# A small last block of an expert's tokens: high and low halves side by side in one stationary operand

## The chip, the core and the metric

The kernel runs on one core of one Trainium2 chip. The metric is the device time of one execution in microseconds (us). TensorE (PE) multiplies, VectorE (DVE) and ScalarE (ACT) compute element by element, GpSimd (POOL) here mostly issues indirect DMAs, and SyncE (SP) issues the other DMAs. Each engine works through its own instruction stream in order and waits on semaphores for the others.

## The reference

Three stages, fp32 throughout: sliding-window attention with sink tokens over 1,536 tokens, a mixture of 8 experts (one expert per token, at most 384 tokens each), and a feed-forward layer with squared ReLU. The change is in the second stage:

```python
expert_idx = np.argmax(x @ w_gate, axis=1)
for i in range(N):                       # capacity = N // E * 2 = 384
    e = expert_idx[i]
    if counts[e] < capacity:
        disp[e, counts[e]] = x[i]; pos[i] = counts[e]; counts[e] += 1; keep[i] = True
h = np.maximum(np.einsum('ecd,edf->ecf', disp, w1), 0.0)   # 512 -> 1024
y = np.einsum('ecf,efd->ecd', h, w2)                       # 1024 -> 512
out[i] = gate_w[i] * y[expert_idx[i], pos[i]]              # for the kept tokens
```

With the reference's inputs the experts 0 to 7 get 290, 123, 98, 163, 117, 165, 92 and 488 tokens; the last is cut to 384.

## The kernel before

**Precision.** A matmul in fp32 is made of passes on rounded operands. Every operand is split into a high part (its value rounded to the matmul format, a copy on ACT) and a low part (the rest, a subtraction on DVE). A product is three passes: high by high, high by low, low by high.

**Blocks.** An expert's tokens are taken in blocks of 128. `body(e, b, ...)` computes block `b` of expert `e`: `g1` makes the hidden layer in two halves of 512 columns (L859; the 128 tokens are the stationary operand, the weights stream past, 512 columns to a matmul), `relu` brings each half to SBUF (L862, ACT), `tr` transposes it by four matmuls (L870) and splits the result (L873 ACT, L874 DVE), and `g2` multiplies by the second weight (L885). A full block is 24 matmuls of `g1` and 24 of `g2`, 512 columns each, with eight transposes between. At the end DVE scales `y` by the gate (L916) and POOL scatters it to `yd` in DRAM (L917).

**Order.** The order of every engine's instructions is written out by hand in `body`. Expert `e`'s first block carries the splitting of expert `e+1`'s weights: sixteen pairs of a copy (L145, ACT) and a subtraction (L146, DVE), spread by the plan `HEAVY`; the eight last stand at the end, behind the preparation `pre` of the next blocks' tokens (L831 PE, L834 ACT, L835 DVE). A raw weight's buffer is free, and SP fetches the next (L139), when its two subtractions are done.

**Later blocks.** `more(e, b)` computes block `b` of 1 and 2 only if the expert has more than `128 b` tokens, which each engine decides by a branch of its own (L927). It splits no weights and prepares the tokens of block `b+1` (if `b+1` is under 3) whether that block is needed or not. Banks of PSUM: three for `h` (`s`), one for the transposes (`pt`), one for `y` (`ot`).

**After the experts.** The feed-forward layer runs in chunks of 512 tokens (L1050, L1106); the last chunk's length is chosen by branches too (L1147).

Of the kernel before, what the change touches and what calls it, by code (L numbers as in the profile page):

```python
# [8 lines left out]
F32 = mybir.dt.float32  # L9
F32R = mybir.dt.float32r  # L10
BF16 = mybir.dt.bfloat16
I32 = mybir.dt.int32
AF = mybir.ActivationFunctionType
ALU = mybir.AluOpType
AX = mybir.AxisListType

P = 128
# [5 lines left out]
LIGHT = (1, 1, 1, 1, 1, 1)  # L23
# [10 lines left out]
def kernel(  # L34
# [15 lines left out]
    nc = tc.nc  # L50
    B, H, S, D = q.shape
    NTOK, DM = out.shape
    E = w_gate.shape[1]
    F = w1.shape[2]
    FF = w_in.shape[1]
    HP = H // 2
    KD = DM // P
    NF = F // P
# [28 lines left out]
    def ps(tag, name):  # L87
        banks[tag].append(banks[tag].pop(0))
        return psum.tile([P, 512], F32, tag=f"b{banks[tag][-1]}", name=name)
# [123 lines left out]
    yd = dram.tile([NTOK, DM + 1], F32, name="yd")  # L213


    W = {0: Weights(0, wx, "x"), 1: Weights(1, None, "y")}
# [60 lines left out]
    ident = const.tile([P, P], F32, name="ident")  # L277
# [43 lines left out]
    if fast:  # L321
# [22 lines left out]
        for g in range(3 if stack else 1):  # L344
            x = own[g * HS : (g + 1) * HS]
            nc.gpsimd.affine_select(x, x, pattern=[[-NS, H], [0, D]], compare_op=ALU.is_ge, fill=0.0, base=0, channel_multiplier=1)
            nc.gpsimd.affine_select(x, x, pattern=[[NS, H], [0, D]], compare_op=ALU.is_ge, fill=0.0, base=NS - 1, channel_multiplier=-1)
    else:
        for j in range(NJ):
            m = ap_.tile([P, S], F32, name=f"m{j}")  # L350
# [268 lines left out]
    def route(n):  # L619
        need(n, "oh")  # L620
        if nblk == 0:
            return
        d = blk[n]
        p_ = ps("lg" if n < NQB - 2 else "s", "pos")
        nc.tensor.matmul(p_[:, :E], tri, d["oh"], start=True, stop=False)
        nc.tensor.matmul(p_[:, :E], ones, runoh, start=False, stop=True)
        nc.gpsimd.tensor_add(runoh, runoh, d["oh"])
        pj = small("pj", E)
        pos = small("pos", 1)
        at = ap_.tile([P, capp], BF16, tag="at", name="at", bufs=2)  # L630

        def places():
            nc.vector.tensor_scalar(at, place, pos, None, op0=ALU.is_equal)
            d["at"] = at

        def take():
            nc.vector.tensor_tensor_reduce(
                out=pj, in0=p_[:, :E], in1=d["oh"], scale=1.0, scalar=0.0, op0=ALU.mult, op1=ALU.add, accum_out=pos
            )
            short.insert(0, places)  # L640

        late.append(take)

    def invert(n):
        if nblk == 0:
            return
        need(n, "at")
        at, wh = blk[n]["at"], blk[n]["wh"]
        p_ = ps("lg" if n < NQB - 2 else "s", "inv")
        for b in range(nblk):  # L650
            for t in range(2):
                nc.tensor.matmul(p_[:, b * E : (b + 1) * E], at[:, b * P : (b + 1) * P], wh[:, t, :], start=t == 0, stop=t == 1)
        late.append(lambda: nc.vector.tensor_add(inv, inv, p_[:, : nblk * E]))
        blk.pop(n)


    XB = 3
    xring = {}
    for b in range(XB):
        for i in range(2):  # L660
            t_ = xring[b, i] = xrp.tile([P, DM + 1], F32, name=f"xb{b}{i}")
# [30 lines left out]
    for n in range(NQB):  # L692
# [5 lines left out]
        fs = (lambda n=n: row(n, 0), lambda n=n: row(n, 1), lambda n=n: route(n), lambda n=n: invert(n))  # L698
# [18 lines left out]
    for u in range(len(units) + PL + 1):  # L717
# [4 lines left out]
        if u < len(units):  # L722
            n, c = units[u]
            b, j = divmod(n, NJ)
# [16 lines left out]
        m, c = divmod(u, HP)  # L741
# [30 lines left out]
    if nblk:  # L772
        src = xrp.tile([P, nblk, E], I32, name="src")
# [5 lines left out]
        p_ = ps("lg", "cnt")  # L779
# [12 lines left out]
        dst = const.tile([P, nblk, E], I32, name="dst")  # L792
# [9 lines left out]
    mp = moe.__enter__()  # L802
# [5 lines left out]
    xT = {}  # L808
# [3 lines left out]
    def x_at(e, b):  # L812
        return xring[min(b, XB - 1), e % 2]

    def gate_at(e, b):
        return gate[2 + b % 2 if b else e % 2]

    def load_x(e, b):
        if e >= E or b >= nblk:
            return  # L820
        nc.gpsimd.indirect_dma_start(
            out=x_at(e, b), out_offset=None, in_=xd[:, :], in_offset=bass.IndirectOffsetOnAxis(ap=src[:, b, e : e + 1], axis=0),
            bounds_check=NTOK - 1, oob_is_err=False,
        )

    def pre(e, b):
        if e >= E or b >= nblk:
            return
        p_ = ps("bg", "xT")
        for c in range(KD):  # L830
            nc.tensor.transpose(p_[:, c * P : (c + 1) * P], x_at(e, b)[:, c * P : (c + 1) * P], ident)  # L831
        xT[e, b] = xTs[min(b, 1)]
        h_, l_ = (x.rearrange("p c n -> p (c n)") for x in xT[e, b])
        nc.scalar.copy(h_, p_)  # L834
        nc.vector.tensor_sub(l_, p_, h_.bitcast(F32))  # L835
        g_ = gate_at(e, b)
        nc.vector.tensor_scalar(g_, x_at(e, b)[:, DM:], 1e-9, None, op0=ALU.add)
        nc.vector.reciprocal(g_, g_)

    def body(e, b, splits, plan, also):  # L840
        xh, xl = xT[e, b]
        wts = W[e]
        splits = list(splits)

        def sp(n):
            for _ in range(n):
                if splits:
                    splits.pop(0)()

        hs = mp.tile([P, F], F32, tag="hs", name="hs", bufs=1)  # L850
        hp = [None, None]

        def g1(half, ks):
            if ks[0] == 0:
                hp[half] = ps("s" if half or b else "iv", "h")
            for kk in ks:
                r = slice(half * 512, half * 512 + 512)
                for m, (a, bb) in enumerate(((xh, wts.h), (xh, wts.l), (xl, wts.h))):
                    nc.tensor.matmul(hp[half], a[:, kk, :], bb[kk][:, r], start=(kk == 0 and m == 0), stop=(kk == KD - 1 and m == 2))  # L859

        def relu(half):
            nc.scalar.activation(hs[:, half * 512 : half * 512 + 512], hp[half], AF.Relu)  # L862

        hT = [None, None]

        def tr(half):
            p_ = ps("pt", "hT")
            for c in range(4):
                o0 = half * 512 + c * P
                nc.tensor.transpose(p_[:, c * P : (c + 1) * P], hs[:, o0 : o0 + P], ident)  # L870
            h_ = mp.tile([P, 512], F32R, tag="hTh", name="hTh", bufs=2)
            l_ = mp.tile([P, 512], F32R, tag="hTl", name="hTl", bufs=2)
            nc.scalar.copy(h_, p_)  # L873
            nc.vector.tensor_sub(l_, p_, h_.bitcast(F32))  # L874
            hT[half] = (h_, l_)

        y = ps("ot", "y")

        def g2(fs):
            for f in fs:  # L880
                h_, l_ = (x[:, (f % 4) * P : (f % 4 + 1) * P] for x in hT[f // 4])
                wh, wl = wts.h[KD + f // 2], wts.l[KD + f // 2]
                r = slice((f % 2) * 512, (f % 2) * 512 + 512)
                for m, (a, bb) in enumerate(((h_, wh), (h_, wl), (l_, wh))):
                    nc.tensor.matmul(y, a, bb[:, r], start=(f == 0 and m == 0), stop=(f == NF - 1 and m == 2))  # L885

        def point(i):
            for f in also.get(i, ()):
                f()

        plan = iter(plan)
        g1(0, [0, 1, 2, 3])
        sp(next(plan))
        relu(0)
        g1(1, [0, 1])
        sp(next(plan))
        tr(0)
        g1(1, [2, 3])
        sp(next(plan))
        relu(1)  # L900
        point(0)
        g2([0, 1])
        sp(next(plan))
        tr(1)
        point(1)
        g2([2, 3])
        point(2)
        sp(next(plan))
        g2([4, 5])
        point(3)  # L910
        g2([6, 7])
        point(4)
        sp(next(plan))
        y_ = mp.tile([P, DM + 1], F32, tag="ys", name="ys", bufs=2)
        nc.gpsimd.tensor_copy(y_.bitcast(I32)[:, DM:], src[:, b, e : e + 1])
        nc.vector.tensor_scalar(y_[:, :DM], y, gate_at(e, b), None, op0=ALU.mult)  # L916
        nc.gpsimd.indirect_dma_start(  # L917
            out=yd[:, :], out_offset=bass.IndirectOffsetOnAxis(ap=dst[:, b, e : e + 1], axis=0), in_=y_, in_offset=None,
            bounds_check=NTOK - 1, oob_is_err=False,
        )  # L920
        sp(len(splits))

    def more(e, b):

        if b >= nblk:
            return
        with tc.If(vals[e] > b * P):  # L927
            if b + 1 >= XB:
                load_x(e, b + 1)
            body(e, b, [], LIGHT, {3: [lambda: pre(e, b + 1)]})  # L930
            more(e, b + 1)

    NPRE = 2
    order = [("i", f) for f in range(NPRE)]
# [53 lines left out]
    vals = []  # L988
    if nblk > 1:
        vals = [nc.values_load(cnt[0:1, e : e + 1], min_val=0, max_val=cap) for e in range(E)]  # L990
# [205 lines left out]
```

## Time and profile before

| | |
|---|---|
| three runs | median 614.15 us (613.76 to 614.29) |
| the profiled execution, its own time | 615.59 us |
| its span, first to last instruction | 613.9 us |
| busy share of the span: PE, DVE, ACT, POOL | 94%, 58%, 48%, 22% |
| mean granted TensorE clock | 0.983 |
| blocks of tokens computed | 14: eight first ones, six later ones |

The profiled execution took 615.59 us, of which 613.9 are its span; 1.7 us lie around it. Matmuls overlap in the array: a row's busy time of a matmul (0.4 us) is longer than the distance from its start to the next one's start, and it is the starts that count time. In a row of the timeline the first two numbers are start and duration, and a bracket at the end tells how long the engine had idled before and what released it.

### The profile page before, as it was taken

The page shows a single profiled execution, that of the slowest core. Times are in us where ns is not written, and L with a number is a line of the kernel's source. Part 1 is how long each engine was busy: PE and PEld are TensorE (multiplying, and loading weights), DVE is VectorE, ACT ScalarE, POOL GpSimd, SP SyncE. Part 2 cuts the span into 40 slices and gives each one's busy share as a digit, 9 for nine tenths or more (in the row PEclk, how much of TensorE's full clock was granted, in tenths as well). Part 3 has the DMA queues.
Part 4 walks back from the last instruction along what each step waited for, and adds up shares of the span by engine and source line. Part 5 has one row for each costly group of instructions (what it writes and reads, how often), then busy time and mean ns, then how long its engine had stood idle before and what let it go on. Part 6 is the DMA issues. An engine that isn't in the chain of part 4 may idle for free. (4 is left out here: it accounts for less than half of the span.)

```text
span 613.9 us, 9330 instructions
## 1 busy us (share of the span) xinstructions
PE 577.7 (94%) x3231; PEld 457.4 (75%) x3231; DVE 353.2 (58%) x833; ACT 296.2 (48%) x649; POOL 135.8 (22%) x235
## 2 busy tenths in 40 slices
PE   8999999969999999999699899999999999999992
PEld 4778778737887787777577677788888888888881
DVE  3788888736439966957652799994223223322221
ACT  4888878616348756747341556563212222222220
POOL 8444554232223422422111100000200000200002
PEclk9999999988999999999899899999999999999997
DMA  9698995445428995857763646621100000100001
GB/s 191 156 219 161 215 198 141 139 138 171 154 60 248 325 309 160 263 208 222 221 218 114 207 146 197 208 84 51 69 0 18 0 1 0 73 0 2 1 0 59
DMA packets 74624, 82.07 MB, mean 134 GB/s; under 512 B 42200, under 2 KB 53464, under 8 KB 74560
## 3 DMA queue, kind: packets, MB, share of 16 engines
q1 hardware_dynamic: 70608, 72.45, 41.6%
q0 software_dynamic: 3952, 8.82, 4.2%
q8 instruction: 34, 0.56, 0.4%
q14 instruction: 30, 0.25, 0.1%
HBM read 69.29 MB, written 16.08 MB: 139 GB/s over the span
## 5 line engine op out<-in xcount | busy, mean ns | idle before, releaser
L1052 ACT ACTIVATE xb<-a 128x512 f32<-128x512 f32 (+1 forms) x48 | 27.5, 573 | 151.7 <-PE a L1050 151.7
L1053 DVE TENSOR_TENSOR xb<-xb 128x512 f32<-128x512 f32 (+1 forms) x48 | 31.7, 661 | 115.6 <-ACT xb L1052 115.5
L1106 PE MATMUL out<-yh,gh 128*128 128x512 f32 (+1 forms) x192 | 77.1, 401 | 0.6 <-ACT gh L1067 0.5
L1106 PE MATMUL out<-yl,gh 128*128 128x512 f32 (+1 forms) x192 | 76.6, 399 | 0.0
L1106 PE MATMUL out<-yh,gl 128*128 128x512 f32 x176 | 70.4, 400 | 2.4 <-DVE gl L1069 2.1
L451 ACT ACTIVATE p<-p,nm 128x260 f32<-128x260 f32 (+2 forms) x96 | 46.8, 489 | 17.3 <-DVE nm L439 16.2
L917 POOL DMA_INDIRECT yd<-ys,dst x14 | 25.5, 1821 | 119.2 <-POOLq L927 51.1
L1075 POOL DMA_INDIRECT out_dram<-raw,tok x12 | 11.7, 976 | 176.0 <-DVE raw L1116 115.3
L1050 PE MATMUL a<-x2Ah,xh 128*128 128x512 f32 (+1 forms) x128 | 48.1, 376 | 0.3 <-PEq L1020 0.3
L1050 PE MATMUL a<-x2Al,xh 128*128 128x512 f32 (+1 forms) x128 | 47.9, 374 | 0.2 <-DVEq L1020 0.2
L1050 PE MATMUL a<-x2Ah,xl 128*128 128x512 f32 (+1 forms) x128 | 47.8, 374 | 0.0
L146 DVE TENSOR_TENSOR yl<-raw,yh 128x512 fp32r<-128x512 f32 x64 | 40.4, 687 | 7.8 <-ACT yh L145 7.8
L1069 DVE TENSOR_TENSOR gl<-xb,gh 128x512 fp32r<-128x512 f32 (+1 forms) x48 | 31.1, 649 | 22.1 <-ACT gh L1067 20.8
L1106 PEld LDWEIGHTS out<-yh,gl 128*128 128x128 f32 x176 | 33.4, 190 | 12.6 <-DVE gl L1069 4.2
L1106 PEld LDWEIGHTS out<-yh,gh 128*128 128x128 f32 (+1 forms) x192 | 35.6, 185 | 9.6 <-ACT gh L1067 0.9
L1106 PEld LDWEIGHTS out<-yl,gh 128*128 128x128 f32 (+1 forms) x192 | 35.5, 185 | 8.4
L1067 ACT CAST gh<-xb 128x512 fp32r<-128x512 f32 (+1 forms) x48 | 28.6, 596 | 24.3 <-DVE xb L1053 24.3
L145 ACT CAST yh<-raw 128x512 fp32r<-128x512 f32 x64 | 35.4, 625 | 2.6 <-PEq L927 1.7
L145 ACT CAST xh<-raw 128x512 fp32r<-128x512 f32 x64 | 36.2, 619 | 0.5 <-DMA raw<-in_moe_w_dram 0.2
L874 DVE TENSOR_TENSOR hTl<-hT,hTh 128x512 fp32r<-128x512 f32 x28 | 19.3, 690 | 28.1 <-ACT hTh L873 25.5
L146 DVE TENSOR_TENSOR xl<-raw,xh 128x512 fp32r<-128x512 f32 x48 | 30.1, 687 | 1.9 <-ACT xh L145 1.8
L526 PE MATMUL ot<-pts,v 128*64 128x128 f32 x352 | 30.1, 286 | 0.5 <-ACT pts L493 0.5
(204 smaller groups left out, 1399.1 us busy)
## 6 DMA issues: line engine op xcount, KB each, us to landing
raw<-in_moe_w_dram SPq DMA_DIRECT2D x64, 512.0 KB, 5.2
raw<-in_moe_w_in_dram SPq DMA_DIRECT2D x16, 512.0 KB, 5.4
raw<-in_moe_w_out_dram SPq DMA_DIRECT2D x8, 1024.0 KB
yd<-zero SPq DMA_DIRECT2D x12, 256.5 KB, 6.3
xd<-x SPq DMA_DIRECT2D x12, 256.5 KB, 5.8
xb<-yd SPq DMA_DIRECT2D x12, 256.5 KB, 3.3
kr<-in_k_dram SPq DMA_DIRECT2D x12, 256.0 KB, 4.7
qr<-in_q_dram SPq DMA_DIRECT2D x12, 256.0 KB, 7.1
```

Of the source, the lines that this page charges most:

```text
L145: (hi or nc.scalar.copy)(self.h[i][:, sl], t[:, sl])
L146: (eng or nc.vector).tensor_sub(self.l[i][:, sl], t[:, sl], self.h[i].bitcast(F32)[:, sl])
L451: nc.scalar.activation(d["p"][:, h, :width], d["p"][:, h, :width], AF.Exp, bias=d["nm"][:, h : h + 1], scale=-1.0, accum_out=d["sm"][:, h ...
L526: nc.tensor.matmul(d["o"][i * D : (i + 1) * D, c * P : (c + 1) * P], vt[b, kb][:, h, :], t_, start=i not in d["started"], stop=False, skip ...
L874: nc.vector.tensor_sub(l_, p_, h_.bitcast(F32))
L917: nc.gpsimd.indirect_dma_start(out=yd[:, :], out_offset=bass.IndirectOffsetOnAxis(ap=dst[:, b, e : e + 1], axis=0), in_=y_, in_offset=None ...
L1050: nc.tensor.matmul(a_[:, :w], a, bb[:, kk, :w], start=(kk == 0 and m == 0), stop=(kk == KD - 1 and m == 2))
L1052: nc.scalar.activation(r_, a_[:, :w], AF.Relu)
L1053: nc.vector.tensor_mul(r_, r_, r_)
L1067: nc.scalar.copy(gh[:, :w], r_)
L1069: nc.vector.tensor_sub(gl[:, : w - k_], r_[:, : w - k_], gh.bitcast(F32)[:, : w - k_])
L1106: nc.tensor.matmul(o, a, bb[:, r], start=(f == 0 and m == 0), stop=(f == NFF - 1 and m == len(prods) - 1))
```

## The change

`more` now asks a second question. A later block that holds more than 64 tokens goes through `body` as before. One with at most 64 goes through the new `packed_body`. It uses that only 64 of the 128 columns of the stationary operand hold tokens: ACT copies the low parts of the 64 tokens into the other 64 columns, beside the high parts, and each weight pass (high, then low) multiplies both at once. The result has the products of the high parts in the upper 64 rows and those of the low parts in the lower 64 rows. Between the two layers the halves are transposed and added by DVE (`tensor_reduce`, L952), put through ReLU into the high part by ACT (L953), and the rest becomes the low part on DVE (L954); at the end ACT copies the lower half of `y`, and DVE adds the upper (L979, L980) and scales (L981). The preparation of a block `b+1` is left out.

```diff
+    def packed_body(e, b):
+        (x, xl), wts = xT[e, b], W[e]
+        nc.scalar.copy(x[:, :, P // 2 :], xl.bitcast(F32)[:, :, : P // 2])
...
+            for kk in ks:
+                for m, bb in enumerate((wts.h, wts.l)):
+                    nc.tensor.matmul(
+                        hp[half], x[:, kk, :], bb[kk][:, r], start=(kk == 0 and m == 0), stop=(kk == KD - 1 and m == 1)
+                    )
...
+        def tr(half):
+            p_ = ps("pt", "hT")
+            for c in range(4):
+                o0 = half * 512 + c * P
+                nc.tensor.transpose(p_[:, c * P : (c + 1) * P], hs[:, o0 : o0 + P], ident)
+            pv = p_.rearrange("p (c t n) -> p c n t", c=4, t=2)
...
+            nc.vector.tensor_reduce(sm, pv, axis=AX.X, op=ALU.add)
+            nc.scalar.activation(t_[:, :, 0, :], sm, AF.Relu)
+            nc.vector.scalar_tensor_tensor(
+                t_[:, :, 1, :], in0=sm, scalar=0.0, in1=t_.bitcast(F32)[:, :, 0, :], op0=ALU.max, op1=ALU.subtract
+            )
...
+        g1(0, [0, 1, 2, 3])
+        keep(0)
+        g1(1, [0, 1, 2])
+        tr(0)
+        g1(1, [3])
+        keep(1)
+        g2([0, 1, 2])
+        tr(1)
+        g2([3, 4, 5, 6, 7])
...
+        nc.scalar.copy(y_[:n, :DM], y[n:, :])
+        nc.vector.tensor_add(y_[:n, :DM], y_[:n, :DM], y[:n, :])
+        nc.vector.tensor_scalar(y_[:n, :DM], y_[:n, :DM], gate_at(e, b)[:n], None, op0=ALU.mult)
...
     def more(e, b):
         if b >= nblk:
             return
         with tc.If(vals[e] > b * P):
-            if b + 1 >= XB:
-                load_x(e, b + 1)
-            body(e, b, [], LIGHT, {3: [lambda: pre(e, b + 1)]})
-            more(e, b + 1)
+            with tc.If(vals[e] > b * P + P // 2) as cmp:
+                if b + 1 >= XB:
+                    load_x(e, b + 1)
+                body(e, b, [], LIGHT, {3: [lambda: pre(e, b + 1)]})
+                more(e, b + 1)
+            with cmp.Else():
+                packed_body(e, b)
```

The first place is ACT's order where expert 3's first block ends and its second begins (`xh` are expert 4's weights being split, `hs` and `hTh` the hidden layer, `xT1h` and `xT1l` the block's tokens). Before:

```order
L145 CAST xh_3642<-raw_75 128x512
L927 COMPARE_AND_BRANCH
L862 ACTIVATE hs<-h 128x512 [waits PE_49,Activation_49]
L873 CAST hTh<-hT 128x512 [waits DVE_49,PE_49]
L862 ACTIVATE hs<-h 128x512 [waits PE_49]
L873 CAST hTh<-hT 128x512 [waits DVE_49,PE_49,Activation_49]
L834 CAST xT1h<-xT 128x512 [waits DVE_49,PE_49,Activation_49]
```

And now the same place; of the packed way's rows, which stand further on in the program:

```order
L927 CAST xT1h<-xT1l 128x4x64 [waits DVE_49,Activation_49]
L942 COPY hs<-h 128x512 [waits PE_49]
L953 ACTIVATE hTh<-hsum 128x4x64 [waits DVE_49]
L942 COPY hs<-h 128x512 [waits PE_49]
L953 ACTIVATE hTh<-hsum 128x4x64 [waits DVE_49]
L979 COPY ys<-y 64x512 [waits DMASW5_49,DMASW3_49,DMASW6_49,DMASW1_49,DMASW7_49,PE_49,Pool_49]
L992 UNCONDITIONAL_BRANCH
```

Before, ACT's first work for the block was `relu`, behind the first half of `g1`; now it is the copy of the low parts, ahead of `g1`. The copy stands behind the eight L145 of the first block. The second place is PE's order between the halves of the same block, from the first transposes to the first matmuls of `g2` (`yh`, `yl` are expert 3's weights). Before:

```order
L870 MATMUL hT<-ident,hs 128x128 [waits Activation_49]
L870 MATMUL hT<-ident,hs 128x128 x3
L859 MATMUL h<-yh_3304,xT1h 128x512
L859 MATMUL h<-yl_3305,xT1h 128x512
L859 MATMUL h<-yh_3304,xT1l 128x512
L859 MATMUL h<-yh_3306,xT1h 128x512
L859 MATMUL h<-yl_3307,xT1h 128x512
L859 MATMUL h<-yh_3306,xT1l 128x512
L885 MATMUL y<-yh_3308,hTh 128x512 [waits DVE_49,Activation_49]
L885 MATMUL y<-yl_3309,hTh 128x512
L885 MATMUL y<-yh_3308,hTl 128x512 [waits DVE_49]
```

And now:

```order
L948 MATMUL hT<-ident,hs 128x128 [waits Activation_49]
L948 MATMUL hT<-ident,hs 128x128 x3
L937 MATMUL h<-yh_3578,xT1h 128x512
L937 MATMUL h<-yl_3579,xT1h 128x512
L965 MATMUL y<-yh_3580,hTh 128x512 [waits DVE_49]
L965 MATMUL y<-yl_3581,hTh 128x512
```

Between the transposes and the first matmul that needs what DVE made of them stood eight matmuls, six of them of `g1` (the first two of `g2` needed only ACT's part); now two stand there. The second half is alike: two matmuls of `g2` between its transposes and the wait.

## Rows read from the trace of the kernel before

**Rows 1.** The profile's chain of waits that ended last, shares by engine and line.
```profile
PE out L1106 20%; PE a L1050 19%; DVE raw L184 1%; PE x2T L969 1%; DMA out_dram<-raw,tok 1%; DVE gl L1069 0%; DVE raw L182 0%; ACT xb L1052 0%; POOLq L1190 0%; POOL out_dram L1075 0%; DVE raw L1112 0%; ACT raw L1111 0%; DVE yl L189 0%; DVE raw L185 0%; DVE xb L1053 0%
```
**Rows 2.** Line L917, one scatter a block: count, duration, first and last start.
```profile
L917 POOL DMA_INDIRECT yd<-ys,dst x14: 983/1904/2652, 156.5 to 336.5; - x14
```
**Rows 3.** Windows of three later blocks: length, then PE, PEld, DVE, ACT, POOL busy, PEclk, DMA.
```profile
165.77:177.84 12.07, 12.07 (x58) 9.80 (x57) 2.41 (x6) 3.93 (x7) 1.19 (x2) 1.00 0.06 23
220.33:233.43 13.10, 12.66 (x62) 10.00 (x60) 7.34 (x14) 5.45 (x11) 2.73 (x2) 1.00 0.67 213
261.25:274.35 13.10, 12.66 (x62) 10.01 (x60) 7.35 (x14) 5.45 (x11) 2.73 (x2) 1.00 0.67 233
```
**Rows 4.** PE's timeline, expert 3's second block: start, duration, engine, line, operation.
```profile
220.33 0.39 PE L859 MATMUL h<-yh,xT1h 128*128 128x512 f32 x1
...
222.90 0.39 PE L859 MATMUL h<-yh,xT1l 128*128 128x512 f32 x1
...
224.53 0.60 PE L870 MATMUL hT<-ident,hs 128*128 128x128 f32 x4
224.88 0.48 PE L859 MATMUL h<-yh,xT1h 128*128 128x512 f32 x1
...
225.20 0.39 PE L859 MATMUL h<-yl,xT1h 128*128 128x512 f32 x1
...
232.59 0.40 PE L885 MATMUL y<-yh,hTl 128*128 128x512 f32 x1
...
233.43 0.50 PE L859 MATMUL h<-xh,xT0h 128*128 128x512 f32 x1 [0.44 <-PEq L927]
```
**Rows 5.** ACT's and DVE's timeline beside it.
```profile
218.24 4.27 ACT L145 CAST xh<-raw 128x512 fp32r<-128x512 f32 x8
223.39 0.60 ACT L862 ACTIVATE hs<-h 128x512 f32<-128x512 f32 x1 [0.87 <-PE h L859]
225.16 0.58 ACT L873 CAST hTh<-hT 128x512 fp32r<-128x512 f32 x1 [1.18 <-PE hT L870]
225.78 0.69 DVE L874 TENSOR_TENSOR hTl<-hT,hTh 128x512 fp32r<-128x512 f32 x1 [0.60 <-ACT hTh L873]
```
**Rows 6.** ACT's timeline at expert 5's second block.
```profile
259.17 4.27 ACT L145 CAST xh<-raw 128x512 fp32r<-128x512 f32 x8
```
**Rows 7.** DVE ahead of expert 0's third block, PE behind it.
```profile
165.23 0.69 DVE L835 TENSOR_TENSOR xT1l<-xT,xT1h 128x512 fp32r<-128x512 f32 x1 [2.56 <-ACT xT1h L834]
177.84 0.39 PE L859 MATMUL h<-yh,xT0h 128*128 128x512 f32 x1
```
**Rows 8.** Groups by line and form: count, busy us, mean ns, idle before.
```profile
L585 ACT COPY x<-xr 128x256 f32<-128x256 f32 x24 | 8.8, 368 | 4.7 <-DVE lt L580 4.6
L495 DVE COPY pts<-pt 128x512 f32<-128x512 f32 x19 | 13.0, 685 | 0.2 <-PE pt L489 0.2
L495 DVE COPY pts<-pt 128x256 f32<-128x256 f32 x4 | 1.7, 419 | 0.3 <-PE pt L489 0.3
L611 DVE TENSOR_REDUCE lg<-lt 128x8 f32<-128x64 f32 x12 | 3.2, 263 | 0.0
L185 DVE SCALAR_TENSOR_TENSOR raw<-raw 128x1024 int32<-128x1024 int32 x16 | 19.6, 1226 | 0.5
```
**Rows 9.** PE's timeline behind its three longest waits from 140 us on.
```profile
296.76 0.50 PE L885 MATMUL y<-yh,hTl 128*128 128x512 f32 x1 [1.83 <-DVE hTl L874]
303.00 0.72 PE L969 MATMUL x2T<-ident,xb 128*128 128x128 f32 x4 [2.77 <-DMA xb<-yd]
...
344.87 0.79 PE L1106 MATMUL out<-yh,gl 128*128 128x512 f32 x1 [2.13 <-DVE gl L1069]
```
**Rows 10.** Windows of the low clock behind the second of them, columns as in Rows 3.
```profile
303.40:306.80 3.40, 3.40 (x13) 2.71 (x12) 0.69 (x1) 0.58 (x1) 0.37 (x2) 0.51 1.01 315
```
**Rows 11.** PE's timeline across the branches at L1147.
```profile
526.50 0.39 PE L1106 MATMUL out<-yh,gl 128*128 128x512 f32 x1
526.72 0.35 PE L1050 MATMUL a<-x2Ah,xh 128*128 128x416 f32 x1
```

More of the change, by code (lines that the diff above doesn't have):

```diff
@@ L921, in body, with g1, keep, g2 @@
         sp(len(splits))
+    def packed_body(e, b):
+        (x, xl), wts = xT[e, b], W[e]
+        nc.scalar.copy(x[:, :, P // 2 :], xl.bitcast(F32)[:, :, : P // 2])
+        hs = mp.tile([P, F], F32, tag="hs", name="hs", bufs=1)
+        hp, hT = [None, None], [None, None]
+        def g1(half, ks):
+            if ks[0] == 0:
+                hp[half] = ps("s", "h")
+            r = slice(half * 512, half * 512 + 512)
+            for kk in ks:
[3 more added lines that the diff above has]
+                    )
+        def keep(half):
+            nc.scalar.copy(hs[:, half * 512 : half * 512 + 512], hp[half])
+        def tr(half):
[4 more added lines that the diff above has]
+            pv = p_.rearrange("p (c t n) -> p c n t", c=4, t=2)
+            sm = mp.tile([P, 4, P // 2], F32, tag="hTl", name="hsum", bufs=2)
+            t_ = mp.tile([P, 4, 2, P // 2], F32R, tag="hTh", name="hTh", bufs=2)
+            nc.vector.tensor_reduce(sm, pv, axis=AX.X, op=ALU.add)
[3 more added lines that the diff above has]
+            )
+            hT[half] = t_.rearrange("p c t n -> p c (t n)")
+        y = ps("ot", "y")
+        def g2(fs):
+            for f in fs:
+                r = slice((f % 2) * 512, (f % 2) * 512 + 512)
+                for m, bb in enumerate((wts.h[KD + f // 2], wts.l[KD + f // 2])):
+                    nc.tensor.matmul(y, hT[f // 4][:, f % 4, :], bb[:, r], start=(f == 0 and m == 0), stop=(f == NF - 1 and m == 1))
+        g1(0, [0, 1, 2, 3])
[7 more added lines that the diff above has]
+        g2([3, 4, 5, 6, 7])
+        n = P // 2
+        y_ = mp.tile([P, DM + 1], F32, tag="ys", name="ys", bufs=2)
+        nc.gpsimd.tensor_copy(y_.bitcast(I32)[:n, DM:], src[:n, b, e : e + 1])
+        nc.scalar.copy(y_[:n, :DM], y[n:, :])
+        nc.vector.tensor_add(y_[:n, :DM], y_[:n, :DM], y[:n, :])
+        nc.vector.tensor_scalar(y_[:n, :DM], y_[:n, :DM], gate_at(e, b)[:n], None, op0=ALU.mult)
+        nc.gpsimd.indirect_dma_start(
+            out=yd[:, :], out_offset=bass.IndirectOffsetOnAxis(ap=dst[:n, b, e : e + 1], axis=0), in_=y_[:n, :], in_offset=None,
+            bounds_check=NTOK - 1, oob_is_err=False,
+        )
```

## The prediction

> **What bounds the kernel now.** I read the chain of waits first, then line L917 and windows over three blocks, then the timelines of PE, ACT and DVE inside one block, and the groups by form for the new operations. The chain that ended last is PE at the feed-forward layer's two matmul lines, with little else [rows 1]: what PE loses or wins among the experts moves the end by as much, as long as PE is the bound there too. It is. Fourteen scatters mean fourteen blocks, so six later ones [rows 2]; the counts that the reference's router gives (290, 163 and 165 tokens at experts 0, 3 and 5; 384 at the last) put at most 64 tokens into exactly three of them: expert 0's third (34), expert 3's second (35) and expert 5's second (37). In their windows PE is busy 12.07 us of 12.07, and 12.66 of 13.10, at full clock [rows 3]. The reader is to see that PE waits for nothing inside these blocks, and that DVE and ACT have time to spare there.
>
> **What is removed.** From 220.33 to 222.90 eleven matmuls start, one every 0.234 us [rows 4]; the 0.39 us of a row overlap and count nothing. A full block has 48 of 512 columns, a packed one 32: 16 x 0.234 = 3.74 us less. Experts 3 and 5 also lose the needless preparation of a third block, four transposes: 0.35 us to the next start, and 0.09 since the first matmul behind transposes takes 0.32 to the next for 0.23 [rows 4], 0.44 together. Their not-taken branch behind the block goes too: 232.59 to 233.43 is 0.84, 0.61 over the pitch [rows 4]. A packed block ends in an unconditional branch, as expert 0's third did, and behind that one PE ran on without a wait [rows 7].
>
> **What is added at the entry.** PE's first matmul now waits for ACT's copy of the low parts. At expert 3 PE could start at 220.33 [rows 4], but ACT is still splitting expert 4's weights: eight copies from 218.24 for 4.27 us, to 222.51 [rows 5]. Before this hid, since ACT's first work for the block, `relu`, came at 223.39, 0.49 after PE's last matmul of the half, with 0.87 us of idle ahead of it. The copy is 256 elements a row: 0.37 us by the ACT copy of 128x256 [rows 8]. With 0.04 for a handover (225.16 + 0.58 to 225.78 [rows 5]) PE starts at 222.92: 2.59 us late. What queues behind the copy on ACT is `keep`, for the transposes, which are later by as much. Expert 5 is the same picture, ACT busy from 259.17 for 4.27 [rows 6] against a block start at 261.25 [rows 3]: 2.60. At expert 0 ACT splits nothing; the low part it copies is ready at 165.92 [rows 7], so PE starts at 165.92 + 0.04 + 0.37 + 0.04 = 166.37 for 165.77 [rows 3]: 0.60. Each restart costs 0.09 more.
>
> **What is added between the layers.** Before, the chain from transposes to the low part ran beside eight matmuls. Now two stand there, twice in a block. The chain: 0.63 from the first transpose to the next engine's start (224.53 to 225.16 [rows 4, 5]); DVE's reduce of 512 elements from PSUM; ACT's ReLU of 256; DVE's rest of 256; three handovers of 0.04. No row shows such a reduce. From below it is 0.26 (a reduce of 64 elements), from above 1.23 (1024 elements); I take 0.69, the DVE copy of 128x512 out of PSUM, which reads as much [rows 8]. The Trainium skill ("VectorE: DVE Perf Modes", "The perf-mode tier table" and "Rules for kernel authors") gives the reduce only the slowest rate of one element a cycle and calls it the slowest operation to have on a hot path; the row of 64 elements is too small to tell rates, and by the rule the sum stays at 0.69 and its lower end is out of reach. ReLU: 0.37, rest: 0.42, as the copies of 256 elements [rows 8]. Sum 0.63 + 0.69 + 0.37 + 0.42 + 0.12 = 2.23. Beside it run the transposes and two matmuls, 0.35 + 0.32 + 0.23 = 0.90 [rows 4]. So PE waits 1.33 us and restarts for 0.09, 1.42 a time, 2.84 a block. From below (both of DVE's at 0.26) the wait is 0.59 shorter, 0.74; from above (reduce at 1.23) 1.87.
>
> **What lies beside.** The end of a packed block is longer by an ACT copy (0.6) and a DVE pass (0.7), both after PE's last matmul. Behind them stand the first three splits of the next expert's weights; PE first needs those engines when twelve matmuls and six more are through, 4.2 us later, and three splits on DVE take 2.1. Hidden; if not, 0.7 us a block. SP's fetches start later by as much, from buffers filled long before. The second question is one more branch an engine; a branch cost PE nothing where it ran on [rows 7].
>
> **The sum.** Expert 3: -3.74 - 0.44 - 0.61 + 2.59 + 0.09 + 2.84 = +0.73. Expert 5: +0.74. Expert 0: -3.74 + 0.60 + 0.09 + 2.84 = -0.21. Together +1.3 us: 13.3 removed, 14.6 given back in waits.
>
> **The clock.** PE's new idle of 2.6 us at two places is among those behind which the granted clock fell: it fell to half behind waits of 2.77 and 2.13 us, and stayed full behind one of 1.83 [rows 9]; behind the first of these it read 0.51 for 3.4 us [rows 10]. Half of 3.4 us is lost at most, 1.7; I take 1.6, as PE has matmuls for most of it. I give each of the two places 4 in 10, so the likeliest case is none or one fall, and I carry half a fall, 0.8.
>
> **The forecast.** The profiled execution took 615.59 us, 613.9 of span and 1.7 around it; 615.59 + 1.3 + 0.8 = 617.7. The median of the runs shown is 1.44 under that execution: 616.2 us, slower by 0.3%. Its own range, none or one fall and 0.15 a wait either way, is 614.5 to 617.9.
>
> **Rivals.**
> - *Two falls of the clock.* 614.15 + 1.3 + 3.2 = 618.7. For it: the two entries look alike in the trace. Against: 1.83 kept the clock, and 2.6 is not far over.
> - *Branches cost.* The program grows, and the packed way lies behind the block it replaces, so each of three jumps to it and four skips of a whole expert (1, 2, 4, 6) goes further. If a far target held PE for another 0.44 us, the largest wait for its own sequencer [rows 4], seven would add 3.1: 618.5 with half a fall left out. Against it: behind the branches at L1147, which pass over two whole variants of the last chunk, PE kept its pitch, 526.50 to 526.72 [rows 11]. The Trainium skill ("Runtime: NRT & Kernel Launch", "Instruction fetch mechanics") says that a taken branch beyond the loaded pages stalls on a fetch of instructions; at L1147 the trace does not agree, so the rival keeps a small chance.
> - *The halves are cheap: faster.* Its place is the wait between the layers, six times. With no fall of the clock and a chain shorter by 0.22 us a time, the change is worth nothing; from 0.42 on it is faster by over 0.2%. At the lower bound (0.59 a time) it is 1.3 - 3.5 = -2.2: 612.0. For it: small operations in the rows are cheap. Against: the reduce must read 512 elements.
> - *The new way is not taken* (the tokens of a block not counted as I do): two questions for one, 614.2.
>
> **How the numbers follow.** Two places at 4 in 10 give none, one or two falls 36, 48 and 16 in 100. The three share 0.71: the forecast has 0.60 (none 0.26, one 0.34), two falls 0.11. Branches have 0.08, cheap halves 0.14, not taken 0.07. 0.2% is 1.23 us, about what a measurement here can tell from no change: slower means over 615.38. Without a fall 615.4 lies on that line, so half of the 0.26 counts as slower, and nearly all of the 0.34: 0.47, with the two slow rivals 0.66. Faster is under 612.92: 0.09 of the cheap halves. The rest, 0.25, is no change. The range for 8 in 10 leaves out the ends: 613.0 to 619.0.
>
> **What would show it.** Right: in the changed profile the first L937 of experts 3 and 5 idles 2.4 to 2.7 us, released by ACT's copy L927; L965 idles about 1.3 us twice in each of three blocks, released by DVE L954; L952 takes about 0.7; the windows of the three blocks are 13.8, 13.8 and 11.9 us from end to start of the neighbours' matmuls. A granted clock of 0.5 behind an entry would show a fall. Wrong: L965 idle under 1.0 (cheap halves), idle put down to PE's own sequencer at L991 or L992 (branches), no L937 at all, or a longer expert 1, 4 or 6, which would mean that the block's longer end is not hidden.

## The result: slower by 1.5%, and the profile after

| | before | after |
|---|---|---|
| median of the timed runs | 613.95 us | 622.2 us (621.4 to 625.7) |
| ratio, 95% interval | 1 | 1.0147, 1.0107 to 1.0187 |
| the profiled execution, its span | 615.59, 613.9 us | 621.4, 619.6 us |

One run of the kernel after, disturbed by a low clock throughout (657.3 us), is left out. The change costs about 9 us; 2.1 were forecast, and 622.2 lies outside the range of 613 to 619.

The chain that ended last is still PE at the same two lines (L1050 is now L1117, L1106 is L1173), to be read against [rows 1]:

```profile
PE out L1173 20%; PE a L1117 19%; DMA out_dram<-raw,tok 1%; DVE raw L184 1%; PE x2T L1036 1%; DVE gl L1136 0%; DVE raw L182 0%; ACT xb L1119 0%; POOLq L1257 0%; DVE raw L1179 0%; ACT raw L1178 0%; POOL out_dram L1142 0%; DVE yl L189 0%; POOLq L1142 0%; DVE raw L185 0%
```

The windows of the three packed blocks, columns as in [rows 3], from PE's first matmul of the block to its first of the next:

```profile
165.33:176.75 11.42, 8.98 (x41) 6.73 (x41) 2.50 (x5) 1.89 (x4) 1.20 (x2) 1.00 0.06 23
222.86:235.89 13.03, 10.52 (x41) 7.85 (x41) 4.45 (x8) 1.89 (x4) 2.71 (x2) 0.87 0.49 170
267.14:280.15 13.01, 10.49 (x41) 7.86 (x41) 4.45 (x8) 1.89 (x4) 2.73 (x2) 0.87 0.48 170
```

A third of PE's work is gone (62 entries in the window before, 41 now), and yet experts 3 and 5 take 13.0 us for 13.1: waits and a clock of 0.87 fill the place. PE's waits from 137 to 340 us (engine and line, waited for: us in total, times, longest):

```profile
PE y L965 <- DVE hTh L954: 7.5, 6, 1.3
PE h L859 <- PEq L991: 5.6, 2, 3.1
PE h L937 <- ACT xT1h L927: 5.5, 3, 2.5
PE x2T L1036 <- DMA xb<-yd: 2.7, 2, 1.8
PE h L859 <- ACTq L991: 2.6, 1, 2.6
```

The first and the third are the waits that the prediction worked out. The second and the fifth it had not: 8.2 us in three waits at L859, the first matmul of an expert. Before, the view had this in their place:

```profile
PE h L859 <- PEq L927: 1.3, 3, 0.4
```

PE's timeline shows where they are: at the skips over the later blocks of experts 2, 4 and 6.

```profile
204.26 0.40 PE L885 MATMUL y<-xh,hTl 128*128 128x512 f32 x1
207.29 0.39 PE L859 MATMUL h<-yh,xT0h 128*128 128x512 f32 x1 [2.63 <-ACTq L991]
...
248.60 0.40 PE L885 MATMUL y<-xh,hTl 128*128 128x512 f32 x1
251.50 0.47 PE L859 MATMUL h<-yh,xT0h 128*128 128x512 f32 x1 [2.50 <-PEq L991]
...
292.86 0.40 PE L885 MATMUL y<-xh,hTl 128*128 128x512 f32 x1
296.32 0.47 PE L859 MATMUL h<-yh,xT0h 128*128 128x512 f32 x1 [3.06 <-PEq L991]
```

From start to start these are 3.03, 2.90 and 3.45 us, where the kernel before has 0.82, 0.55 and 0.55: 7.5 us more. The trace also records PE's own branch at the end of an expert (not counted as busy, so in no view above): 5.89 us at 245.43 and 6.47 at 289.67, against 0.3 at most others. PE's matmuls run 3.2 us behind its sequencer (248.60 - 245.43), so the first 3.2 us of a branch are hidden. A transfer of 16 KB on the instruction queue begins 3.53 us after the first of these branches and 3.89 us after the second. The page's table of DMA queues, of before and then of after, counts more of them:

```profile
q8 instruction: 34, 0.56, 0.4%
```

```profile
q8 instruction: 40, 0.66, 0.4%
```

Some of the loss comes back at the last expert, whose first block takes 17.9 us for 21.9: PE comes later to the transfers and splits that it waited for there ([rows 9] has two of these waits).

Inside expert 3's block, to be read with [rows 4, 5], PE's, ACT's and DVE's rows:

```profile
222.86 0.58 PE L937 MATMUL h<-yh,xT1h 128*128 128x512 f32 x1 [2.46 <-ACT xT1h L927]
...
228.42 0.40 PE L937 MATMUL h<-yl,xT1h 128*128 128x512 f32 x1
230.11 0.50 PE L965 MATMUL y<-yh,hTh 128*128 128x512 f32 x1 [1.29 <-DVE hTh L954]
...
222.30 0.41 ACT L927 CAST xT1h<-xT1l 128x256 fp32r<-128x256 f32 x1
...
229.18 0.42 ACT L953 ACTIVATE hTh<-hsum 128x256 fp32r<-128x256 f32 x1 [2.14 <-DVE hsum L952]
...
228.46 0.69 DVE L952 TENSOR_REDUCE hsum<-hT 128x256 f32<-128x512 f32 x1 [3.38 <-PE hT L948]
229.63 0.42 DVE L954 SCALAR_TENSOR_TENSOR hTh<-hsum,hTh 128x256 fp32r<-128x256 f32 x1 [0.48 <-ACT hTh L953]
```

The entry's copy, the reduce and the two waits are close to the forecast. The clock, forecast to fall behind each entry with 4 in 10, fell behind both, to 0.50 and 0.51 of full speed, the lower of its two levels (1.2 for 2.4 GHz):

```profile
223.10:226.50 3.40, 3.40 (x9) 2.61 (x9) 1.98 (x4) 0.04 (x1) 2.71 (x2) 0.50 0.95 323
267.40:270.90 3.50, 3.50 (x10) 2.69 (x10) 1.96 (x4) 0.24 (x1) 2.73 (x2) 0.51 0.96 322
```

### The profile page after: what moved, and what is told of

It is laid out like the page before. It is cut to its first block, busy times and chain, and to the rows that moved or that the text cites. A ratio compares the mean times of both kernels' runs of the same rounds, so it can differ in the third digit from the quotient of the medians.

```text
span 619.6 us, 9239 instructions
## 1 busy us (share of the span) xinstructions
PE 566.2 (91%) x3175; PEld 446.9 (72%) x3175; DVE 355.6 (57%) x836; ACT 296.1 (48%) x653; POOL 138.9 (22%) x235
## 5 line engine op out<-in xcount | busy, mean ns | idle before, releaser
L1173 PE MATMUL out<-yh,gh 128*128 128x512 f32 (+1 forms) x192 | 77.2, 402 | 1.0 <-issue 0.5
L1173 PE MATMUL out<-yl,gh 128*128 128x512 f32 (+1 forms) x192 | 76.6, 399 | 0.0
L1173 PE MATMUL out<-yh,gl 128*128 128x512 f32 x176 | 70.5, 401 | 2.4 <-DVE gl L1136 2.2
L1117 PE MATMUL a<-x2Ah,xh 128*128 128x512 f32 (+1 forms) x128 | 48.1, 376 | 0.3 <-PEq L1087 0.3
L1117 PE MATMUL a<-x2Al,xh 128*128 128x512 f32 (+1 forms) x128 | 47.9, 374 | 0.2 <-DVEq L1087 0.2
L1117 PE MATMUL a<-x2Ah,xl 128*128 128x512 f32 (+1 forms) x128 | 47.8, 374 | 0.0
L1173 PEld LDWEIGHTS out<-yh,gh 128*128 128x128 f32 (+1 forms) x192 | 35.6, 186 | 10.4 <-issue 1.3
L1173 PEld LDWEIGHTS out<-yh,gl 128*128 128x128 f32 x176 | 33.4, 190 | 12.6 <-DVE gl L1136 4.6
L917 POOL DMA_INDIRECT yd<-ys,dst x11 | 21.5, 1951 | 90.5 <-POOLq L991 29.5
L1173 PEld LDWEIGHTS out<-yl,gh 128*128 128x128 f32 (+1 forms) x192 | 35.6, 185 | 8.4
L145 ACT CAST xh<-raw 128x512 fp32r<-128x512 f32 x64 | 36.2, 618 | 0.8 <-PEq L991 0.5
L145 ACT CAST yh<-raw 128x512 fp32r<-128x512 f32 x64 | 35.3, 623 | 0.2 <-ACTq L991 0.2
L821 POOL DMA_INDIRECT xb<-xd,src x24 | 27.7, 1155 | 11.4 <-issue 4.6
```

The source lines that it names most:

```text
L145: (hi or nc.scalar.copy)(self.h[i][:, sl], t[:, sl])
L821: nc.gpsimd.indirect_dma_start(out=x_at(e, b), out_offset=None, in_=xd[:, :], in_offset=bass.IndirectOffsetOnAxis(ap=src[:, b, e : e + 1], ...
L917: nc.gpsimd.indirect_dma_start(out=yd[:, :], out_offset=bass.IndirectOffsetOnAxis(ap=dst[:, b, e : e + 1], axis=0), in_=y_, in_offset=None ...
L1117: nc.tensor.matmul(a_[:, :w], a, bb[:, kk, :w], start=(kk == 0 and m == 0), stop=(kk == KD - 1 and m == 2))
L1173: nc.tensor.matmul(o, a, bb[:, r], start=(f == 0 and m == 0), stop=(f == NFF - 1 and m == len(prods) - 1))
```

## The experiments

Theory 1: the packed ways lengthen the code that the skips jump over, PE's instructions at the target are not there yet, and their fetch outlasts PE's lead. Theory 2, the rival: the waits and clock falls in the packed blocks are the whole loss. Each run has its ratio to the kernel before on the same chip, with a 95% interval; 0.1% is 0.6 us.

**e1_grown: the code without its use.**
```diff
-            with tc.If(vals[e] > b * P + P // 2) as cmp:
+            with tc.If(vals[e] > b * P) as cmp:
```


> The kernel after, with the inner question the same as the outer one (more than b x 128 tokens), so the packed way is in the program and is never taken: every block is a full one, as before. Theory 1 (jumps over more instructions hold PE): the long gaps of PE behind the skips of experts 2, 4 and 6 stay (3.0, 2.9, 3.5 us for 0.8, 0.5, 0.5 before, 7.5 us together), of which the last expert may give back up to 4 us in its waits: 617.5 to 621.5 us. Theory 2 (the waits and clock falls inside the three packed blocks are the loss): no gap over 1 us at those skips, 613.5 to 615.5 us.

Measured: 617.3 us, 1.0061 (1.0041 to 1.0081), just under the 617.5 that theory 1 gave. No packed block runs, yet the gaps at the skips of experts 2, 4 and 6 are 2.99, 1.98 and 1.36 us. Unused code alone costs 0.6%. Theory 2 cannot be the whole.

**e2_few_ways: the use without most of the code.**
```diff
+    WAYS = ((0, 2), (3, 1), (5, 1))
...
+            if (e, b) not in WAYS:
+                plain()
```


> The packed way stands in the program only where these tokens take it (expert 0's third block, the second of experts 3 and 5); the skips of experts 1, 2, 4 and 6 pass over as much as before. The packed blocks run as in the kernel after. Theory 1: the three gaps are back under 1 us, and 622.2 - 7.5 = 614.7, plus up to 4 us that the last expert's waits take back: 614.7 to 618.7 us. Theory 2: 621 to 623 us, as the blocks are the same.

Measured: 616.6 us, 1.0065 (1.0040 to 1.0090). The gaps are 0.55 at all four skips, and PE's waits for the packed blocks are those of after:

```profile
PE y L965 <- DVE hTh L954: 7.5, 6, 1.3
PE h L937 <- ACT xT1h L927: 5.6, 3, 2.5
```

So the loss has two halves: 0.65% from the blocks, as much again from the code that is jumped over; together they give 1.3% of after's 1.5%.

**e5_pad20, e6_pad80, e7_pad240: only PE's code, and only its length.**
```diff
+            if b == 2 and e in (1, 2, 4, 6):
+                never = ps("ot", "never")
+                for _ in range(20):          # 80, 240
+                    nc.tensor.matmul(never, zb[:, :P], zb, start=True, stop=True)
```


> The kernel before, with 20 more matmuls (40 rows of PE's program) at the end of the third block of experts 1, 2, 4 and 6, which no token reaches: they never run, and only lengthen what the four skips pass over, from some 236 rows to some 276. No other engine's program grows. Theory 1 in its sharper form: PE's instructions come in pieces of 16 KB, one for each 246 to 265 PE rows in straight code; a jump that lands two pieces further holds PE, one that lands in the same or the next does not. 276 rows land two pieces on in about 8 cases of 100: no gap over 1 us at the skips or one, 613.5 to 616 us. Rival (each row passed over costs): 40 of the 160 rows that the kernel after adds, so a quarter of 7.5 us, spread evenly: 615.5 us. Theory 2: 613.5.

> The same with 80 matmuls (160 rows), as many PE rows as the packed ways of an expert: skips of some 396 rows. Theory 1: lands two pieces on in about half of the cases, two or three gaps of 2 to 3 us at the skips of experts 1, 2, 4, 6, 616 to 620 us as e1_grown (617.3). A rival within it, that the growth of the other engines' programs (ACT, DVE, POOL) is what holds: no gap, 613.5. Theory 2: 613.5.

> The same with 240 matmuls (480 rows): skips of some 716 rows, always two to four pieces on. Theory 1 with pieces: a stall at each of the four skips, of about the size of those in e6_pad80 (2 to 3 us each, as one fetch each), 8 to 12 us of gaps, of which the stages behind take some back: 619 to 624 us. Rival (cost by rows passed over): 3 times the gaps of e6_pad80, over 625 us. Theory 2: 613.5.

Measured: 614.1, 616.6 and 616.4 us; 1.0006 (0.9986 to 1.0026), 1.0043 (1.0020 to 1.0065), 1.0048 (1.0023 to 1.0073). The records give, at each skip, the branch's duration and behind the slash PE's gap from start to start, in us:

| skip of expert | 1 | 2 | 4 | 6 |
|---|---|---|---|---|
| before | 0.35 / 0.55 | 3.80 / 0.82 | 0.34 / 0.55 | 0.31 / 0.55 |
| after | 0.32 / 0.55 | 0.31 / 3.03 | 5.89 / 2.90 | 6.47 / 3.45 |
| e5_pad20 | 0.34 / 0.55 | 0.42 / 0.55 | 0.32 / 0.55 | 0.32 / 0.55 |
| e6_pad80 | 5.11 / 2.10 | 6.16 / 3.14 | 0.33 / 0.55 | 5.01 / 1.99 |
| e7_pad240 | 5.52 / 2.57 | 5.84 / 2.83 | 4.80 / 1.78 | 5.41 / 2.38 |
| e13_pad240_thin (below) | 3.56 / 0.55 | 3.82 / 0.80 | 3.61 / 0.59 | 4.50 / 1.50 |

40 rows more cost nothing, 160 stall three skips, 480 all four, and a stall doesn't grow with the distance: it is one fetch or none. In every long branch of the table the gap is the branch less 3.0 us; up to 3.56 us nothing shows beyond the 0.55 of a short one. That PE's code alone grew, and no other engine's, settles whose fetch it is.

e7's time missed: 619 to 624 us were expected, from the right number of stalls. A stall can come back where PE otherwise waits for DVE and ACT a little later. The stall at expert 4 came back whole: from PE's last matmul before that skip to its last before expert 6's, e7 takes 40.93 us with the stall and e6 40.92 without. The stall at expert 2 did not: to expert 4's skip, e6 takes 43.5 us and e7 43.3, where e5_pad20 takes 40.9; there the clock fell as well.

At expert 2 the kernel after (and e1_grown) stalls behind a short branch: the first weight load at the target starts at once (204.78 us), its matmul only at 207.29, and a 16 KB transfer begins 0.14 us behind the load. What sets whether the branch or this place pays was not settled.

**e13_pad240_thin, e14_before_thin: why the same jump costs nothing elsewhere.** At the last chunk (L1147 before) PE's branch at 522.71 took 3.62 us and PE kept its pitch; a later one, 3.26 us, has no matmul behind it. There DMA is nearly idle (a busy share of 0.02).
```diff
+            n = 64 if self.thin else 512          # thin: experts 2 to 7
             nc.sync.dma_start(
-                t.rearrange(...), x
+                t.rearrange(...)[:, :, :n], x...[:, :, :n]
```


> e7_pad240 with an eighth of the bytes fetched of the weights of experts 2 to 7 (64 of each 512 columns; the rest of a tile keeps what an earlier fetch left), so that the DMA engines are nearly idle at the skips of experts 2, 4 and 6, and less busy at expert 1's. The jumps go as far as in e7_pad240. Theory 1a (the piece of instructions waits in the DMA queues behind the weights: 2.4 to 3.5 us from the branch to its transfer at a busy share of 0.57 to 0.83, against 0.93 to 1.0 at L1147 at 0.02): branches of 3.3 to 4 us for 4.8 to 5.8, which PE's queued matmuls hide as at L1147, gaps of 0.5 to 1 us for 1.8 to 2.8. Theory 1b (the distance alone sets it): branches and gaps as in e7_pad240.

> The kernel before with the same eighth of the weights' bytes, to read the times of e13 against: branches at the four skips of 0.3 us and gaps of 0.55, as in the kernel before; its span within 1 us of e13's by theory 1a, 5 to 7.5 us under it by 1b.

Measured, one run each: 614.9 and 613.0 us, spans 613.2 and 611.3, 1.9 apart, of which 1.2 are the gaps of e13's second and fourth skips. From branch to landing, the windows of e7_pad240 at its four skips and at the last chunk's branch (the last two columns are the DMA engines' busy share and GB/s):

```profile
186.01:191.53 5.52, 3.60 (x20) 2.70 (x17) 4.45 (x11) 5.14 (x10) 0.00 (x0) 1.00 0.64 212
201.39:207.23 5.84, 3.58 (x20) 2.69 (x17) 4.78 (x12) 5.22 (x10) 0.00 (x0) 1.00 0.84 317
244.70:249.50 4.80, 3.58 (x20) 2.68 (x17) 3.75 (x10) 4.43 (x9) 0.00 (x0) 1.00 0.51 189
285.62:291.03 5.41, 3.59 (x20) 2.69 (x17) 4.34 (x11) 5.03 (x10) 0.00 (x0) 1.00 0.58 180
522.84:526.46 3.62, 3.62 (x18) 2.89 (x17) 0.79 (x2) 1.35 (x3) 0.00 (x0) 1.00 0.02 5
```

and those of e13_pad240_thin:

```profile
185.52:189.08 3.56, 3.56 (x20) 2.68 (x17) 2.50 (x8) 3.19 (x7) 0.00 (x0) 1.00 0.13 31
200.29:204.11 3.82, 3.58 (x20) 2.69 (x17) 2.76 (x8) 3.45 (x7) 0.00 (x0) 1.00 0.23 73
241.19:244.80 3.61, 3.59 (x20) 2.70 (x17) 2.54 (x8) 3.23 (x7) 0.00 (x0) 1.00 0.10 23
282.14:286.64 4.50, 3.56 (x19) 2.67 (x17) 3.46 (x9) 4.14 (x9) 0.00 (x0) 1.00 0.57 185
```

The distance is the same; with most of the weights' bytes gone the branch takes 3.6 to 3.8 us, close to the last chunk's, and PE's lead hides it but for 0.25 us at the second skip. The fourth skip is a control within the run: the feed-forward layer's weights, not thinned, still keep DMA at 0.57 there, and it stalls, though for 1.50 us where e7 has 2.38 at 0.58. The records split a branch in two: from its start to the 16 KB transfer's start 3.09, 3.46, 2.42 and 2.84 us in e7 (in the order of its skips), 1.22, 1.23, 1.24 and 2.19 in e13, 0.9 to 1.0 at the last chunk; from there to the branch's end 2.3 to 2.7 everywhere in these two runs. So the fetch waits for its transfer while the weights stream, as theory 1a has it; that it waits in a queue of the DMA engines and not for the memory behind them is not shown. The busy share alone does not set the wait: at before's branch of 202.18 us it was 1.04, and the transfer began after 1.32 us.

**e3_early_low: no copy at the entry.**
```diff
+        if b and (e, b) in WAYS:          # in pre; xw is the high part's tile, 64 columns wider
+            nc.vector.tensor_copy(xw[:, :, : P // 2], l_.bitcast(F32)[:, :, : P // 2])
...
-        nc.scalar.copy(x[:, :, P // 2 :], xl.bitcast(F32)[:, :, : P // 2])
```


> The kernel after, with the low parts of a later block's first 64 tokens put beside the high ones already in pre, by DVE (one more DVE copy of 256 elements a later block; the high part's tile is 192 wide). ACT's copy at the entry of a packed block goes, and with it the first matmul's wait for it. Both theories: waits of 2.6, 2.6 and 0.6 us at the entries go and the clock stays full there (13.0 us of window for experts 3 and 5 become 9.8 to 10.4). Theory 1: the three gaps at the skips stay, so 622.2 - 5.8 to 622.2 - 9 less what the last expert's waits take back: 613 to 619 us. Theory 2: 612.5 to 614.5, under the kernel before by what the removed matmuls are worth.

Measured: 617.2 us, 1.0081 (1.0051 to 1.0112). The waits at the entries are gone, and the windows of experts 3 and 5 are 12.6 us, not 9.8 to 10.4: both theories missed that DVE, too, is still splitting weights there. In its timeline the first reduce stands behind four splits, and PE waits 2.4 us for what follows it:

```profile
223.70 2.48 DVE L146 TENSOR_TENSOR xl<-raw,xh 128x512 fp32r<-128x512 f32 x4
226.10 0.68 DVE L957 TENSOR_REDUCE hsum<-hT 128x256 f32<-128x512 f32 x1
```

**e4_more_cover: four and six matmuls beside the chain.**
```diff
-        g1(1, [0, 1, 2]); tr(0); g1(1, [3]); keep(1); g2([0, 1, 2]); tr(1); g2([3, 4, 5, 6, 7])
+        g1(1, [0, 1]); tr(0); g1(1, [2, 3]); keep(1); g2([0]); tr(1); g2([1, 2, 3, 4, 5, 6, 7])
```


> The kernel after, with other work behind the transposes of a packed block: four matmuls of the first layer behind the first transposes (two before), six of the second layer behind the second (two). Chain 2.23 us as the rows give it; cover 0.35 + 0.32 + 3 x 0.234 = 1.37 the first time, so 0.86 of wait, and 1.84 the second time with the transposes 0.3 us later, so 0.4: 1.26 for 2.66 a block, 4.2 us less over three blocks. Both theories: 618 us, with the gaps at the skips still there; up to 621 if the last expert's waits take it back. A rival that ACT's keep, not the cover, sets the wait: 622.

Measured: 619.9 us, 1.0106 (1.0073 to 1.0140). The six waits fell by 4.2 us, as worked out:

```profile
PE y L965 <- DVE hTh L954: 3.3, 6, 0.8
```

The stalls at the skips are still there (3.30, 3.32 and 3.87 us), and the time is between the two figures expected.

**e8_combined, e9_combined_all, e10_before_tail, e11_combined_no_tail, e12_combined_second: what the halves are worth.** e8 joins e2, e3 and e4, and:
```diff
+            tail = body(e, 0, splits, HEAVY if g < E else LAST, also, 4 if e in (3, 5) else 0)
             more(e, 1)
+            for f in tail:          # the last four splits
+                f()
```


> e2, e3 and e4 together, and for experts 3 and 5 the last four splits of the next expert's weights behind the packed block instead of ahead of it (in e3_early_low DVE's reduce stood behind four of them until 226.10, 1.2 us after it could start, and ACT's queue was free by then). From e2_few_ways: entries 2.6, 2.6 and 0.8 us less, waits between the layers 1.2 less a block, no clock falls at the entries (1.5 each): 616.4 - 6.0 - 3.6 - 3.0 = 603.8 us if nothing takes it back; with up to 4 us taken back by the last expert's waits 608. Rival: the stream of weights sets the pace of these stages and takes most of it back: 611 to 614 us.

> e8_combined with the packed way back at every later block of every expert, as in the kernel after: only the stretches that the skips pass over are longer (some 396 PE rows for 236). Theory 1: stalls of 2 to 3.5 us at two to four of the skips of experts 1, 2, 4 and 6, as in the kernel after and in e6_pad80, so 609.5 + 3 to 6 = 612 to 616 us. Rival (with PE's other waits gone, the weights' stream behind takes it all back): 609.5 to 611.

> The kernel before with nothing but the last four splits of experts 4's and 6's weights moved behind the second block of experts 3 and 5, as in e8_combined; no packed way at all. If the gain of e8_combined came from that move, this is 609.5 to 611 us; if it comes from the packed blocks, 612.5 to 614.5, since a full block hides the splits behind 18 matmuls as it is.

> e8_combined with the four splits ahead of the packed block again. DVE's first reduce of experts 3 and 5 then stands behind four splits (e3_early_low: it began 1.2 us late at expert 3, and 1.2 at expert 5 where it could have begun at 266.1), and with four matmuls more of cover PE comes to it earlier by 0.5: 1.2 to 2 us more at each, 612 to 614 us.

> e8_combined with the packed way at the second block of every expert (and at expert 0's third): skips of some 316 PE rows. By pieces of 256 rows a jump over 316 lands two pieces on in 60 of 256 cases, so one stall of 2 to 3 us among the four skips, 610 to 613 us; none is as likely as two. Rival (cost by rows): half of what e9_combined_all shows.

| | us | ratio, 95% interval | gaps at the skips |
|---|---|---|---|
| e8_combined | 609.5 | 0.9931 (0.9910 to 0.9952) | four of 0.55 |
| e9_combined_all | 615.0 | 1.0025 (1.0007 to 1.0042) | 0.55, 3.04, 3.37, 3.96 |
| e10_before_tail | 613.5 | 1.0000 (0.9986 to 1.0014) | four of 0.55 |
| e11_combined_no_tail | 610.4 | 0.9952 (0.9934 to 0.9970) | four of 0.55 |
| e12_combined_second | 609.8 | 0.9947 (0.9929 to 0.9965) | four of 0.55 |

The three packed blocks of e8, windows as above:

```profile
164.60:174.68 10.08, 8.96 (x40) 6.64 (x41) 3.00 (x6) 1.90 (x4) 1.20 (x2) 1.00 0.07 26
217.53:227.91 10.38, 9.09 (x42) 6.55 (x40) 5.03 (x9) 2.00 (x5) 1.24 (x2) 1.00 0.49 159
256.76:266.95 10.19, 9.02 (x42) 6.64 (x41) 5.00 (x9) 2.00 (x5) 1.23 (x2) 1.00 0.46 157
```

Packing pays once its waits are gone and the jumps stay short: the windows of experts 3 and 5 are 2.7 and 2.9 us shorter than in e5_pad20 (13.08 both), expert 0's 2.0, of which 0.6 goes into a later entry; and the clock is full in all three. Another 1.0 us each comes back at experts 4 and 6, whose first blocks take 14.4 us for 13.4, PE waiting there for ACT behind the moved splits. What is left of the 7.6 us is 4.9; the feed-forward layer begins 4.8 us earlier than in e5_pad20, whose blocks are those of before (both counted from expert 0's second block). The time falls by 0.7%; at 609.5 us it lies above the 603.8 to 608 expected and below the rival's 611. With all ways in the program (e9) 0.9% is lost again to the jumps, and it is slower than before: the code, not the blocks, is the larger sum there. The move of four splits alone is worth nothing (e10). In e8 it is worth little too: without it (e11) the time is 610.4 us where 612 to 614 were expected, the intervals overlap, and expert 3's second block and expert 4's first take 24.9 us together for e8's 24.8. e12 has the packed way at every expert's second block, skips of 316 rows: one stall was expected and none came. Two of its branches took 2.98 and 2.23 us; their transfers had begun 0.54 us after the branch and 0.21 before it, earlier than behind any branch that stalled, and PE's lead hid the rest. e8 and e12 compute the same for any routing; only which small blocks are packed depends on where the ways stand.

## Why the prediction was wrong, step by step

- **What is removed.** Right. In e2_few_ways expert 5's packed block, at full clock, takes 11.45 us where a full one takes 13.08 (e5_pad20): 1.63 less; the terms behind the entry give 3.74 + 0.44 + 0.61 - 2.84 = 1.95. The missing 0.3 is in the waits between the layers and the restarts behind them and behind the entry.
- **The entry.** Right: 2.86 us from start to start, 2.63 over the pitch, for 2.59 forecast; 0.79 at expert 0 for 0.60.
- **Between the layers.** Right in kind, 0.2 us a block too low: 1.69 and 1.62 us from start to start, 1.46 and 1.39 over the pitch, for 1.33; the restart behind each costs another 0.10 for 0.09. The reduce took 0.69, as the copy of 128x512 had; it was the one cost with a wide bound.
- **The block's end.** Right: expert 1's window is 13.26 us, as before.
- **The clock.** Its price was right (seven or eight matmuls at 0.43 us for 0.234, some 1.5 us a fall for 1.6), its chance unproven: it fell behind both entries here and in e4, behind one of two in e2, and behind one of two gaps of 2.78 us in e11 (0.50 from 263.40 us for 3.4 us). The forecast has it at the entries alone. It also fell behind 11 of the 15 stalls of 2.7 us and more at the skips of after, e1, e3, e4, e6, e7 and e9 (none of the three in after's profiled execution), so part of what a stall costs is the clock behind it.
- **Branches. This step failed.** "The second question is one more branch an engine; a branch cost PE nothing where it ran on" counted the branches and not the code that they pass over. The rival that had it was priced at 0.44 us a jump and given 0.08, for the row at L1147 [rows 11]. That row is a jump that did pay: its branch took 3.62 us with DMA at 0.02, and 3.8 us of queued matmuls hid it (the branch began at 522.71, the last matmul before its target at 526.50). Among the experts the lead is 3.2 us, DMA is at 0.5 to 0.9, and branches that wait for a fetch take 4.4 to 7.5 us (after, e1, e3, e4, e6, e7, e9). Measured, 2.2, 2.35 and 2.9 us over before's gaps at three skips, and the sign that the prediction had named for this rival: idle put down to PE's sequencer at L991. The three jumps to the packed way, which the rival counted too, show no gap of their own. One record of before pointed there and was not read: PE's branch at 202.18 took 3.80 us, hidden but for 0.27. The Trainium skill ("Runtime: NRT & Kernel Launch", "Instruction fetch mechanics") says that a taken branch beyond the loaded pages waits for a fetch; I held one row against it, misread, and the runs agree with the page: 276 rows passed over gave no stall, 396 three of four, 716 four.
- **The sum.** In e2's trace the packed blocks of experts 0, 3 and 5 cost 0.14, 2.56 (with a fall of the clock) and 1.00 us against e5_pad20's, 3.7 together, where the forecast's terms with one fall give 2.9. In the timed runs, without the jumps (e2), the change costs 0.65%, 4.0 us (2.5 to 5.5), for 2.1 forecast, below that interval. With the jumps it costs 9.0; e2's 4.0 and the 2.6 to 3.7 us of e6 and e1 account for 6.6 to 7.7 of it, within the intervals.

## What to carry to other kernels

Code that is skipped is not free: before a way is added inside a conditional, count the instructions that the usual jump then passes over, on the engine that is the bound, and compare the branch's own duration with that engine's lead (here 3.2 us among the experts), in a stretch with the same DMA load. A zero cost read elsewhere holds only under that stretch's load and lead. And when work on the bound engine is cut, list what its new first operand stands behind on each other engine: moving the copy off ACT only showed the next queue, DVE's.

## What the runs showed of the hardware

- PE's instructions arrive in transfers of 16 KB; in straight code the starts of seven successive ones (348.2 to 523.7 us, before) lie 225 to 292 PE rows apart, 257 on average. Jumps over 276 and 316 rows didn't stall, jumps over 396 did at three of four skips (after, e1, e3, e4, e6, e9), over 716 at four.
- A branch that waits for such a fetch takes 3.3 to 3.8 us with DMA at 0.02 to 0.23 and 4.5 to 5.8 at 0.51 to 0.84 (e7, e13); the part that grows is the time until its transfer begins, 0.9 to 3.5 us. Of e7's four stalls (7.4 us of gaps beyond 0.55) 0.5% of the time, some 3 us, arrived at the end.
- A VectorE reduce of pairs of elements 64 apart, 128x512 out of PSUM, took 0.69 us, as long as the plain copy [rows 8].
